# Fourier mixing and a maxout layer on one core: mirror rows stored by plain transfers, table columns in another order, and more units in split form

## The chip, the cores and the metric

The kernel runs on one core of a Trainium2 chip. The core has a matrix engine (TensorE, PE in the profile; its weight loads are listed as PEld), a vector engine (VectorE, DVE), a scalar engine (ScalarE, ACT), a general engine (GpSimd, POOL) and a sync engine (SyncE, SP), which here only issues transfers. DMA queues move data between the large memory and the on-chip memory; SP, ACT and POOL each issue transfers of their own. Each engine works through its own list of instructions in order and waits on semaphores for the others. Times are device microseconds of one execution; lower is better.

## What is computed

```python
def _attn_ref(x):                         # x: (8, 3072, 256)
    X = np.fft.fft(x, axis=1)
    X = np.fft.fft(X, axis=2)
    return X.real.astype(np.float32)

def _moe_ref(x, w1, w2, w3, w_out):       # x: (24576, 256), w1..w3: (256, 768), w_out: (768, 256)
    h = np.maximum(np.maximum(x @ w1, x @ w2), x @ w3)
    return (h @ w_out).astype(np.float32)
```

The result of the first, taken as 24576 rows of 256, goes into the second; the output is 24576 rows of 256 floats.

## The kernel before

The eight sequences (batches, b = 0 to 7) are worked on one after the other, each overlapped with the next. The transform along the sequence is made for half of the rows k only: for such a row the kernel holds an even part tE and an odd part tO (columns of two [128 x 1536] arrays), and the row k is formed with their sum, the mirrored row 3072 - k with their difference. So every column of tE and tO gives two output rows, called plus and minus, with two hidden arrays hp and hm.

**Making tE and tO (class Mix).** `s` multiplies the loaded x by a small table, `y` and `z` bring the product through the large memory into another layout (`db`, `yb`), `x` (method x0) fills in a column, and `k` makes 512 columns (a bank) of tE or tO from sine and cosine tables. `_parts` (lines 39 to 48) lists the pieces of a bank: each piece is one matmul with weights of its own, and its columns in the tables are 32 rows apart in k. `v` brings the first row of tO back as an array `vb`, spread over all partitions. These pieces for batch b + 1 are hung by a plan on the units of batch b.

**Units.** A batch has three blocks of 512 columns, and a block has six hidden chunks of 128 (NJC): 18 units, u = 0 to 17, and g = 18 b + u. The loop at line 855 goes through the units. A unit makes one chunk of hp and of hm: the largest of three products. One of them is taken out as a common term, so two remain, each with an even and an odd matmul.

- An ordinary unit: `begin` issues four matmuls (lines 490, 491) into two banks, ACT takes the positive part of one (`stmp`, line 503), DVE the maximum of both (hp, line 504). `finish` adds two matmuls by which both banks turn from plus to minus (line 497), and ACT and DVE do the same again (hm).
- A split unit (`is_split`): its third product is made two units earlier by `third` (lines 815 to 828) from one even and one odd matmul; ACT scales the odd one (line 823), DVE makes the even sum (line 824, which also reads vb), and POOL forms plus3 and minus3 (line 828). `begin` then issues two matmuls into one bank (lines 835, 836) and DVE takes the maximum with plus3 (line 837); `finish` adds one matmul to the same bank (line 497), and DVE takes the maximum with minus3 (line 849).

The order of both is what line 869 sets: if the unit before is a split one, it is finished ahead of this unit's begin; otherwise behind it. After begin and finish come `third` for two units ahead, `scatter`, ten steps of the output stage (`l2_some(10)`), and then the plan's pieces. Before the change the split units are the odd ones from g = 7 on: nine in a batch, six in batch 0.

**Output stage.** `l2_block` works on the block before in four pieces (sub 0 to 3) of 128 columns, 60 steps in six units. A piece gathers plus and minus in one bank `po` (lines 513, 536), and DVE adds the linear part (line 541) into a tile `ot` of [128 x 512], of which there are six: plus in the left half, minus in the right. SP stores the plus rows, two or three plain transfers a piece by `_runs`. The minus rows of a piece, whose place runs backwards, are written on POOL by an indirect transfer, one row per partition (line 622), with row numbers that `rows` computes in batch 0, and a one-element memset behind it (line 626). `l2_last` does the last block, where all other work is done: pieces in the order 3, 0, 1, 2, each with its stores spread over ACT, SP and POOL, and the last piece copied in two halves (line 574).

Of the kernel before, what the change touches and what calls it, by code (L numbers as in the profile page):

```python
# [29 lines left out]
def _runs(slot):  # L30

    if slot == 11:
        return [(0, 48, 0), (48, 96, 16), (96, 128, 15 + 32 * 64)]
    t, u = divmod(slot, 3)
    edge, r = 96 - 32 * u, 4 * t + 1 + u
    return [(0, edge, r + 32 * 32 * u), (edge, 128, r + 1)]


def _parts(g):

    cols = [(r, 96 * (r - 1), 96 if r < 15 else 64, 0) for r in range(1, 16)]
    cols += [(0, 1408, 48, 0), (16, 1456, 48, 0), (15, 1504, 32, 64)]
    done = []
    for (r, c, wd, _) in cols:
        a, z = max(c, 512 * g), min(c + wd, 512 * g + 512)
        if a < z:
            done.append(((r - 1) % 16 if r < 16 else 16, a - 512 * g, z - a))
    return done
# [3 lines left out]
def kernel(  # L52
# [62 lines left out]
    rows_m = consts.tile([128, 12 * B], INT32, tag="rows_m")  # L115
    mark = consts.tile([1, 1], FP32, tag="mark")
# [49 lines left out]
    kvec = gen.tile([128, NHALF + 1], FP32, tag="kvec")  # L166
    kv = kvec[:, 0:1440].rearrange("p (r j) -> p r j", j=96)

    def ramp(r):
        n = {0: 6, 6: 5, 11: 4}[r]  # L170
        iota(kv[:, r:r + n, :], [[1, n], [32, 96]], base=r + 1)

    dvec = gen.tile([128, 128], FP32, tag="dvec")
    for c, (s0, s1) in enumerate(FIRST):
        for h in range(2):
            load_x(0, s0, s1, h)
        if c == 0:
            iota(dvec, [[1, 128]])
        elif c < 3:
            ramp((0, 6)[c - 1])  # L180
# [12 lines left out]
    ramp(11)  # L193
    iota(kvec[:, 1408:1504].rearrange("p (r j) -> p r j", r=2), [[16, 2], [32, 48]])
    iota(kvec[:, 1504:NHALF], [[32, 32]], base=15 + 32 * 64)
    iota(kvec[:, NHALF:NHALF + 1], [[0, 1]], base=NHALF)
# [72 lines left out]
    q = gen.tile([128, NHALF + 1], FP32, tag="q")  # L269
# [118 lines left out]
    class Mix:  # L388
# [72 lines left out]
        def k(self, which, g, evict=nc.scalar.copy):  # L461

            tab = (te_tab, to_tab)[which]
            ps2 = ps_f.tile([128, 512], FP32, name="ps2", tag="ps")
            for (i, c0, wd) in _parts(g):
                nc.tensor.matmul(ps2[:, c0:c0 + wd], self.col(i, which),  # L466
                                 tab[:, g * 512 + c0:g * 512 + c0 + wd], start=True, stop=True)
# [38 lines left out]
    def stored(st, mine, others):  # L506
        for group in others:
            tc.declare_no_dep(st.ins, group=group, reason="each store has rows of its own")
        tc.add_to_no_dep_group(mine, st.ins)
# [7 lines left out]
    def l2_block(b, blk, hp, hm, te, to):  # L517

        base = b * S
        for sub in range(4):  # L520
            slot = blk * 4 + sub
            cp = slice(slot * 128, slot * 128 + 128)
            sp = slice(sub * 128, sub * 128 + 128)
            if sub % 2 == 0:
                pl = ps_f.tile([128, 512], FP32, name="pl", tag="ps")
                for i in range(2):
                    ci = (slot + i) * 128
                    nc.tensor.matmul(pl[:, i * 256:(i + 1) * 256], te[:, ci:ci + 128],  # L528
                                     gw[:, 0:256], start=True, stop=True)
                    yield  # L530
                even = even_pool.tile([128, 512], FP32, name="even", tag="even")
# [3 lines left out]
            ot = out_pool.tile([128, 512], FP32, name="ot", tag="ot")  # L535
# [5 lines left out]
            nc.vector.tensor_tensor(  # L541
                out=ot.rearrange("p (h c) -> p h c", h=2),
                in0=po.rearrange("p (h c) -> p h c", h=2),
                in1=lin.unsqueeze(1).to_broadcast([128, 2, 256]), op=ALU.add)
            lo = 1 if slot == 11 else 0
            waiting.append((b * 12 + slot, lo, ot))
            for (p0, p1, k0) in _runs(slot):
                row = base + k0
                stored(nc.sync.dma_start(out=out[row: row + 32 * (p1 - p0 - 1) + 1: 32, :],
                                         in_=ot[p0:p1, 0:256]), "direct", ("scattered",))  # L550

    def l2_last(hp, hm, te, to, flipped):

        base = (B - 1) * S
        ter, tor = flipped
        for sub in (3, 0, 1, 2):
# [4 lines left out]
            ot = out_pool.tile([128, 512], FP32, name="ot", tag="ot")  # L561
            for (h, tev, tov, wo, hid) in (
                    (0, te[:, cp], to[:, cp], gw[:, 256:512], lambda jc: hp[:, jc, sp]),
                    (1, ter[:, sm], tor[:, sm], gw[:, 512:768], lambda jc: hm[:, jc, sm])):
                if h == 0 or sub == 2:
# [7 lines left out]
                if sub == 2:  # L573
                    nc.vector.tensor_copy(out=ot[:, h * 256:(h + 1) * 256], in_=ph)
            if sub != 2:
                nc.vector.tensor_copy(out=ot, in_=po)
            stores = [(p0, p1, base + k0, 0) for (p0, p1, k0) in _runs(slot)]
            for (p0, p1, k0) in _runs(slot):
                if k0 == 0:
                    p0, k0 = 1, 32  # L580
                stores.append((128 - p1, 128 - p0, base + S - k0 - 32 * (p1 - p0 - 1), 256))
            for k, (p0, p1, row, c) in enumerate(stores):
                eng = (nc.scalar, nc.sync, nc.gpsimd)[(k + (sub == 2)) % 3]
                stored(eng.dma_start(out=out[row: row + 32 * (p1 - p0 - 1) + 1: 32, :],
                                     in_=ot[p0:p1, c:c + 256]), "direct", ("scattered",))

    def l2_mid():
# [20 lines left out]
        for _ in l2_hidden(po[0:B, 0:256], lambda jc: hmid[:, jc, :]):  # L608
            pass
        ot = out_pool.tile([128, 512], FP32, name="ot", tag="ot")  # L610
        nc.vector.tensor_copy(out=ot[0:B, 0:256], in_=po[0:B, 0:256])
        stored(nc.sync.dma_start(out=out[NHALF: NHALF + S * (B - 1) + 1: S, :],
                                 in_=ot[0:B, 0:256]), "direct", ("scattered",))
# [4 lines left out]
    def scatter():  # L618

        while waiting:  # L620
            at_row, lo, ot = waiting.pop(0)
            stored(nc.gpsimd.indirect_dma_start(  # L622
                out, bass.IndirectOffsetOnAxis(
                    ap=rows_m[0:128 - lo, at_row: at_row + 1], axis=0),
                ot[lo:128, 256:512], None), "scattered", ("scattered", "direct"))
            nc.gpsimd.memset(mark, 0.0)
# [60 lines left out]
    m.c(1, 7)  # L687
# [9 lines left out]
    def rows():  # L697

        rows_f = gen.tile([128, 12 * B], FP32, tag="rows_f")
        iota(rows_f.rearrange("p (b t u) -> p b t u", t=4, u=3), [[S, B], [-4, 4], [-1025, 3]],  # L700
             base=S - 1, cm=-32)
        rows_v = rows_f.rearrange("p (b r) -> p b r", r=12)
        adj = gen.tile([128, 12], FP32, tag="adj")
        adv = adj.rearrange("p (t u) -> p t u", u=3)
        four = pidx.to_broadcast([128, 4])
        pool = nc.gpsimd
        for u in range(3):
            scal(adv[:, :, u], four, float(96 - 32 * u), ALU.is_ge, 3071.0, ALU.mult, eng=pool)
        low = gen.tile([128, 2], FP32, tag="low")
        scal(low[:, 0:1], pidx, 47.0, ALU.is_ge, 1520.0, ALU.mult, eng=pool)  # L710
        scal(low[:, 1:2], pidx, 95.0, ALU.is_ge, -511.0, ALU.mult, eng=pool)
        scal(low[:, 0:1], low[:, 0:1], 2031.0, ALU.add, eng=pool)
        pool.tensor_tensor(out=adj[:, 11:12], in0=low[:, 0:1], in1=low[:, 1:2], op=ALU.add)
        pool.tensor_tensor(out=rows_v, in0=rows_v,
                           in1=adj.unsqueeze(1).to_broadcast([128, B, 12]), op=ALU.add)
        pool.tensor_copy(rows_m, rows_f)

# [5 lines left out]
    out_pool = ctx.enter_context(tc.tile_pool(name="outbuf", bufs=6))  # L723
# [45 lines left out]
    for (u, fn) in ((0, lambda: table(2, 512, 1024)), (0, lambda: m.c(7, 16)),  # L769
# [6 lines left out]
                    (3, lambda: table(2)), (3, lambda: table(0)), (5, rows),  # L776
# [28 lines left out]
    def is_split(g):  # L805
        return g % 2 == 1 and 7 <= g < B * UNITS
# [118 lines left out]
```

## Time and profile before

| | |
|---|---|
| median of three runs | 394.9 us (394.51 to 395.22) |
| the profiled execution, its own time | 395.75 us |
| its span in the profile | 393.8 us |
| clock granted to TensorE, mean | 0.996 |
| matrix engine busy | 377.7 us in 2710 instructions |
| vector / scalar / general engine busy | 315.0 / 263.0 / 332.9 us |
| transfers | 54.20 MB, 66901 packets |

The page of a profile gives the busy time of each engine, the chain of work that ended last (followed back from the last instruction, with its shares by engine and line), the costliest groups of instructions (line, engine, operation, output <- inputs, shape, count | busy us, mean ns of one | idle time of the engine before them and who ended it), and the DMA queues (packets, MB, share of the time of 16 DMA engines). A timeline row has start and length in us, engine, line, operation, count of merged instructions, and in brackets how long the engine had been idle and what ended that. Matmuls are pipelined: one of 512 columns is listed with 0.38 us, and the next starts earlier than that. Vector operations overlap a little in the same way. L150 is line 150 of the kernel.

### The profile page before, as it was taken

How to read it: one execution, taken by the hardware profiler on the slowest of the kernel's cores; microseconds unless marked ns; L12 is line 12 of the kernel's file. 1: busy time of each engine (PE TensorE's matmuls, PEld its weight loads, DVE VectorE, ACT ScalarE, POOL GpSimd, SP SyncE). 2: the span in 40 equal slices, each digit the busy share in tenths (PEclk: the TensorE clock that was granted, in tenths of full speed). 3: DMA queues.
4: the chain of work that ended last, by engine and by line, in shares of the span. 5: the costliest groups of instructions: out<-in, count | busy, mean ns of one | idle time of the engine just before them, and what ended most of it. 6: DMA issues, size and time to landing. Idle time of an engine off the chain costs nothing.

```text
span 393.8 us, 8383 instructions
## 1 busy us (share of the span) xinstructions
PE 377.7 (96%) x2710; PEld 235.9 (60%) x2759; DVE 315.0 (80%) x530; ACT 263.0 (67%) x476; POOL 332.9 (85%) x432
## 2 busy tenths in 40 slices
PE   6698999999999999999999999999999999999994
PEld 2354566566665666565665666556665666666673
DVE  7788897788687788788787888877887887887972
ACT  6877788677766887577867787578866447435420
POOL 8985698979978899889988899889977898869993
PEclk9999999999999999999999999999999999999998
DMA  7999576585838776495767876495333553321234
GB/s 115 159 194 183 131 191 146 114 191 150 161 102 144 190 153 144 117 206 137 137 150 120 210 132 160 118 206 124 108 108 101 131 147 90 94 77 47 90 96 131
DMA packets 66901, 54.20 MB, mean 138 GB/s; under 512 B 32702, under 2 KB 62556, under 8 KB 66003
## 3 DMA queue, kind: packets, MB, share of 16 engines
q0 software_dynamic: 24368, 26.53, 35.5%
q1 hardware_dynamic: 41978, 26.72, 27.0%
q8 instruction: 21, 0.34, 0.4%
q10 hardware_dynamic: 512, 0.43, 0.4%
q14 instruction: 22, 0.18, 0.1%
HBM read 36.95 MB, written 30.81 MB: 172 GB/s over the span
## 4 chain that ended last, share of the span: by engine, by line
PE 84%; DMA 4%; DVE 4%; ACT 3%; issue 2%; POOL 2%; SPq 1%; DVEq 0%; ACTq 0%; POOLq 0%
PE po L513 30%; PE pse L497 12%; PE pse L490 8%; PE pse L491 7%; PE po L536 4%; PE d L821 4%; PE pse L835 4%; PE e L819 3%; PE ps L466 3%; PE pse L836 3%; PE pl L528 2%; PE ps L401 2%; DMA yb<-db 2%; DMA xt<-in_x_dram 2%; ACT tb L405 1%
## 5 line engine op out<-in xcount | busy, mean ns | idle before, releaser
L503 ACT ACTIVATE stmp<-pse 128x512 bf16<-128x512 f32 x150 | 89.6, 600 | 66.1 <-PE pse L497 50.9
L622 POOL DMA_INDIRECT out_dram<-ot,rows_m x92 | 102.4, 1113 | 17.9 <-issue 8.8
L828 POOL TENSOR_TENSOR plus<-even,odd 128x512 bf16<-128x512 f32 x69 | 87.8, 1272 | 32.9 <-DVE even L824 32.7
L828 POOL TENSOR_TENSOR minus<-even,odd 128x512 bf16<-128x512 f32 x69 | 87.5, 1268 | 0.0
L513 PE MATMUL po<-wout_bf,hp 128*128 128x256 bf16 x576 | 86.1, 273 | 0.4
L837 DVE SCALAR_TENSOR_TENSOR hp<-pse,plus 128x512 bf16<-128x512 f32 x69 | 47.6, 689 | 46.5 <-PE pse L836 13.9
L513 PE MATMUL po<-wout_bf,hm 128*128 128x256 bf16 x576 | 78.6, 273 | 0.0
L513 PEld LDWEIGHTS <-hp 128*128 128x128 bf16 x576 | 56.4, 98 | 26.1
L497 PE MATMUL pse<-tO,gd_all 128*128 128x512 bf16 x217 | 70.5, 379 | 1.1 <-DVE hp L504 0.2
L513 PEld LDWEIGHTS <-hm 128*128 128x128 bf16 x576 | 56.4, 98 | 16.3
L541 DVE TENSOR_TENSOR ot<-po,even 128x512 f32<-128x512 f32 x92 | 62.7, 681 | 0.0
L504 DVE TENSOR_TENSOR hp<-pse,stmp 128x512 bf16<-128x512 f32 x75 | 51.4, 685 | 10.1 <-ACT stmp L503 8.7
L490 PE MATMUL pse<-tE,g_all 128*128 128x512 bf16 x148 | 56.0, 379 | 1.9 <-DVE tE L468 0.5
L504 DVE TENSOR_TENSOR hm<-pse,stmp 128x512 bf16<-128x512 f32 x75 | 51.5, 687 | 7.4 <-ACT stmp L503 4.1
L824 DVE SCALAR_TENSOR_TENSOR even<-vb,wcol,e 128x512 f32<-128x512 bf16 x69 | 50.8, 737 | 0.0
L491 PE MATMUL pse<-tO,g_all 128*128 128x512 bf16 x131 | 49.6, 379 | 0.2 <-issue 0.2
L849 DVE SCALAR_TENSOR_TENSOR hm<-pse,minus 128x512 bf16<-128x512 f32 x69 | 47.0, 681 | 0.7
L823 ACT ACTIVATE odd<-d 128x512 f32<-128x512 f32 x69 | 41.3, 598 | 6.2
L134 ACT COPY xt<-xt 64x762 bf16<-64x762 bf16 (+1 forms) x48 | 40.2, 838 | 1.1
L497 PEld LDWEIGHTS <-gd_all 128*128 128x128 bf16 x219 | 21.3, 97 | 22.2 <-issue 4.1
L536 PE MATMUL po<-gw,tO 128*128 128x512 bf16 x85 | 32.3, 380 | 0.0
L405 ACT CAST tb<-ps 128x512 bf16<-128x512 f32 x38 | 20.5, 588 | 14.1 <-PE ps L401 14.1
(175 smaller groups left out, 475.7 us busy)
## 6 DMA issues: line engine op xcount, KB each, us to landing
xt<-in_x_dram POOLq DMA_DIRECT2D x14, 384.0 KB, 8.4
out_dram<-ot SPq DMA_DIRECT2D x55, 96.0 KB
out_dram<-ot SPq DMA_DIRECT2D x64, 64.0 KB
db<-tb SPq DMA_DIRECT2D x21, 192.0 KB
vb<-vd SPq DMA_DIRECT2D x23, 128.0 KB
xt<-in_x_dram POOLq DMA_DIRECT2D x7, 400.0 KB, 6.9
xt<-in_x_dram POOLq DMA_DIRECT2D x7, 368.0 KB, 6.1
out_dram<-ot SPq DMA_DIRECT2D x62, 32.0 KB
```

The costliest lines, as they stand in the source:

```text
L490: nc.tensor.matmul(pse[:, 0:n], g_all[:, jc, 2 * i, :], te, start=True, stop=False)
L491: nc.tensor.matmul(pse[:, 0:n], g_all[:, jc, 2 * i + 1, :], to, start=False, stop=True)
L497: nc.tensor.matmul(pse, gd_all[:, jc, i, :], to, start=False, stop=True, skip_group_check=True)
L503: nc.scalar.activation(out=stmp[:, 0:n], in_=pses[0][:, 0:n], func=AX.Relu)
L504: nc.vector.tensor_tensor(out=dst, in0=src3, in1=stmp[:, 0:n], op=ALU.max)
L513: nc.tensor.matmul(po, hcols(jc), wout_bf[:, jc * 256:(jc + 1) * 256], start=False, stop=(jc == NJC - 1), skip_group_check=True)
L536: nc.tensor.matmul(po, to[:, cp], gw[:, 256:768], start=True, stop=True)
L541: nc.vector.tensor_tensor(out=ot.rearrange("p (h c) -> p h c", h=2), in0=po.rearrange("p (h c) -> p h c", h=2), in1=lin.unsqueeze(1).to_br ...
L622: stored(nc.gpsimd.indirect_dma_start(out, bass.IndirectOffsetOnAxis(ap=rows_m[0:128 - lo, at_row: at_row + 1], axis=0), ot[lo:128, 256:51 ...
L824: nc.vector.scalar_tensor_tensor(out=even3, in0=vb, scalar=wcol[:, jc:jc + 1], in1=e3, op0=ALU.mult, op1=ALU.add)
L828: nc.gpsimd.tensor_tensor(out=dst, in0=even3, in1=odd3, op=op)
L837: nc.vector.scalar_tensor_tensor(out=dst, in0=pse2, scalar=0.0, in1=sums[g][0], op0=ALU.max, op1=ALU.max)
```

## The change

Three things are changed.

1. *Order of the table's columns.* Each bank of 512 columns consists of four pieces of 128. In a piece, partition p of the output stage has in its first 96 places one residue of k (48 of a upper half, then 48 of a lower half, ascending in each), in the last 32 another one. Each `k` bank now has 8, 8 and 9 matmuls instead of 6, 6 and 8. The single leftover column is row 0 instead of row 1536.
2. *Stores.* A block's four pieces go into one buffer of [128 x 8 x 256], plus rows in places 0 to 3, minus rows in places 7 to 4, so that rows that follow one another in the output lie side by side. There are three such buffers (`obuf` and the two halves of `kq`, which holds the angles at the start). When the fourth piece is done, SP stores the plus rows with four transfers (six in the third block), and POOL the minus rows with two (three) plain transfers whose destination goes backwards in its inner dimension of 48 (or 16). The indirect transfers, `rows`, the memset and the six `ot` tiles are gone. In the last block the order of the pieces is 1, 2, 3, 0; the first three are stored together with twelve transfers, the last in two halves of four, all shared out over ACT, SP and POOL in turn.
3. *Split units.* Units 0, 4 and 8 of batches 1 to 7 are split as well: twelve in a batch, 90 in all instead of 69.

```diff
 def _parts(g):
-    cols = [(r, 96 * (r - 1), 96 if r < 15 else 64, 0) for r in range(1, 16)]
...
+    done = [(12 + i - 1, slice(128 * i + 96, 128 * i + 128)) for i in range(4)]
+    for i in range(4 if g < 2 else 3):
+        done.append((4 * g + i, slice(128 * i, 128 * i + 96)))
+    if g == 2:
+        done += [(16, slice(384, 480, 2)), (15, slice(385, 480, 2))]
     return done
...
-    kvec = gen.tile([128, NHALF + 1], FP32, tag="kvec")
+    kq = gen.tile([128, 4096], FP32, tag="kq")
+    kvec, q = kq[:, 0:NHALF + 1], kq[:, 2048:2049 + NHALF]
+    def ramp(g):
+        kv = kvec[:, 512 * g:512 * g + 512].rearrange("p (s c) -> p s c", s=4)
+        n = 4 if g < 2 else 3
+        iota(kv[:, 0:n, 0:96].rearrange("p s (a j) -> p s a j", a=2),
+             [[1, n], [-1536, 2], [32, 48]], base=4 * g + 1 + 1536)
+        iota(kv[:, :, 96:128].rearrange("p s (a j) -> p s a j", a=2),
+             [[1, 4], [-512, 2], [32, 16]], base=12 + 1024 * g + 512)
...
+    def back(v):
+        return v.rearrange("(a j) r d -> a j r d", a=2)[:, ::-1]
+    def stores_plus(b, blk, buf, s0=0, s1=4):
+        mine, v = rows_of(b)
+        n = s1 if blk < 2 else min(s1, 3)
+        for a in range(2):
+            j = 48 - 48 * a
+            yield v[j:j + 48, 4 * blk + 1 + s0:4 * blk + 1 + n, :], buf[48 * a:48 * a + 48, s0:n, :]
+            j = 32 * blk + 16 - 16 * a
+            yield v[j:j + 16, 12 + s0:12 + s1, :], buf[96 + 16 * a:112 + 16 * a, s0:s1, :]
+        if n < s1:
+            yield mine[784:784 + 46 * 16 + 1:16, :], buf[0:47, 3, :]
+            yield mine[16:16 + 47 * 16 + 1:16, :], buf[48:96, 3, :]
+    def stores_minus(b, blk, buf):
+        mine, v = rows_of(b)
+        n = 4 if blk < 2 else 3
+        r = 32 - 4 * blk
+        yield back(v[0:96, r - n:r, :]), buf[0:96, 8 - n:8, :]
+        yield back(v[64 - 32 * blk:96 - 32 * blk, 17:21, :]), buf[96:128, 4:8, :]
+        if n < 4:
+            yield back(mine[NHALF:S - 15:16, :].unsqueeze(1)), buf[0:96, 4:5, :]
...
             nc.vector.tensor_tensor(
-                out=ot.rearrange("p (h c) -> p h c", h=2),
-                in0=po.rearrange("p (h c) -> p h c", h=2),
+                out=buf[:, sub:8 - sub:7 - 2 * sub, :], in0=po.rearrange("p (h c) -> p h c", h=2),
                 in1=lin.unsqueeze(1).to_broadcast([128, 2, 256]), op=ALU.add)
...
+        for (dst, src) in stores_plus(b, blk, buf):
+            store(nc.sync, dst, src)
+        waiting.extend(stores_minus(b, blk, buf))
...
-        for sub in (3, 0, 1, 2):
+        for sub in (1, 2, 3, 0):
...
+                    if sub == 3:
+                        stores = [*stores_plus(B - 1, 2, buf, 1, 4),
+                                  *stores_turned(B - 1, buf, 1, 4)]
+                for k, (dst, src) in enumerate(stores):
+                    store((nc.scalar, nc.sync, nc.gpsimd)[k % 3], dst, src)
...
         while waiting:
-            at_row, lo, ot = waiting.pop(0)
-            stored(nc.gpsimd.indirect_dma_start(
...
-            nc.gpsimd.memset(mark, 0.0)
+            store(nc.gpsimd, *waiting.pop(0))
...
     def is_split(g):
-        return g % 2 == 1 and 7 <= g < B * UNITS
+        if g % 2 == 0:
+            return UNITS <= g < B * UNITS and g % UNITS in (0, 4, 8)
+        return 7 <= g < B * UNITS
```

`store` issues one transfer and declares that it has no dependence on the stores of the other two queues. `stores_turned` gives the minus rows of the last block, which `l2_last` computes in mirrored order, so that its transfers run forwards.

More of the change, by code (lines that the diff above doesn't have):

```diff
@@ L504, in unit_out, with store @@
         nc.vector.tensor_tensor(out=dst, in0=src3, in1=stmp[:, 0:n], op=ALU.max)
[L506 to L509, printed above, removed]
+    def store(eng, dst, src):
+        st = eng.dma_start(out=dst, in_=src)
+        for other in (nc.sync, nc.scalar, nc.gpsimd):
+            if other is not eng:
+                tc.declare_no_dep(st.ins, group=f"rows {other.engine}",
+                                  reason="each store has rows of its own")
+        tc.add_to_no_dep_group(f"rows {eng.engine}", st.ins)
@@ L609, in l2_mid @@
             pass
-        ot = out_pool.tile([128, 512], FP32, name="ot", tag="ot")
+        ot = even_pool.tile([128, 512], FP32, name="even", tag="even")
         nc.vector.tensor_copy(out=ot[0:B, 0:256], in_=po[0:B, 0:256])
-        stored(nc.sync.dma_start(out=out[NHALF: NHALF + S * (B - 1) + 1: S, :],
-                                 in_=ot[0:B, 0:256]), "direct", ("scattered",))
+        store(nc.sync, out[0: S * (B - 1) + 1: S, :], ot[0:B, 0:256])
     l2_queue = []
@@ L695 @@
     angle()
[L697 to L716, printed above, removed]
     ps_s_cm.__exit__(None, None, None)
@@ L767, in turn @@
         mirror(b, *EIGHTHS[ch])
[L769 removed]
+    for (u, fn) in ((0, lambda: table(2, 512, 1024)),
                     (0, lambda: next(second)), (0, lambda: next(first)),
```

95 lines of the change are left out of this document (38 added, 57 removed).

## The prediction, made before the changed kernel had run

> **What bounds the kernel now.** I read the page first: busy times, the chain of waits, the groups.
>
> ```profile
> span 393.8 us, 8383 instructions
> ...
> PE 377.7 (96%) x2710; PEld 235.9 (60%) x2759; DVE 315.0 (80%) x530; ACT 263.0 (67%) x476; POOL 332.9 (85%) x432
> ...
> PE 84%; DMA 4%; DVE 4%; ACT 3%; issue 2%; POOL 2%; SPq 1%; DVEq 0%; ACTq 0%; POOLq 0%
> ...
> L622 POOL DMA_INDIRECT out_dram<-ot,rows_m x92 | 102.4, 1113 | 17.9 <-issue 8.8
> L828 POOL TENSOR_TENSOR plus<-even,odd 128x512 bf16<-128x512 f32 x69 | 87.8, 1272 | 32.9 <-DVE even L824 32.7
> ```
>
> TensorE has work 96% of the span and carries 84% of the chain. GpSimd is next at 85%, a third of it the scattered mirror stores (1.11 us each), but it is hardly on the chain. Then a view by stretches: one steady batch, and one with the end of batch 0 and most of batch 1 (columns: length, then busy time and count for PE, weight loads, DVE, ACT, POOL, then clock, DMA share, GB/s).
>
> ```profile
> 212.44:257.35 44.91, 44.59 (x320) 27.95 (x325) 36.56 (x57) 32.92 (x59) 39.67 (x49) 1.00 0.70 151
> 45.00:122.62 77.62, 76.57 (x556) 48.03 (x566) 62.54 (x98) 57.88 (x102) 67.86 (x82) 1.00 0.64 146
> ```
>
> A batch takes 44.91 us, of which TensorE idles 0.32: removed matmul time is removed span, as long as no wait opens in its place. DVE looks free for 8.3 us in a batch. That is an average, so I looked at DVE where the new split units land, around the end of one batch (units 17 and 0, then 1).
>
> ```profile
> 157.05 0.69 DVE L837 SCALAR_TENSOR_TENSOR hp<-pse,plus 128x512 bf16<-128x512 f32 x1 [0.41 <-PE pse L836]
> 157.83 0.69 DVE L504 TENSOR_TENSOR hm<-pse,stmp 128x512 bf16<-128x512 f32 x1
> 158.43 0.74 DVE L824 SCALAR_TENSOR_TENSOR even<-vb,wcol,e 128x512 f32<-128x512 bf16 x1
> 159.09 0.68 DVE L541 TENSOR_TENSOR ot<-po,even 128x512 f32<-128x512 f32 x1
> 159.69 0.68 DVE L849 SCALAR_TENSOR_TENSOR hm<-pse,minus 128x512 bf16<-128x512 f32 x1
> 160.29 0.68 DVE L504 TENSOR_TENSOR hp<-pse,stmp 128x512 bf16<-128x512 f32 x1
> ```
>
> In order: hp of unit 17, hm of 16, the even sum for unit 1, the output add, hm of 17, hp of unit 0. From 157.83 on DVE is back to back, one start each 0.60 us (0.65 for the even sum), and hp of unit 0 starts when DVE gets to it, not when TensorE delivers. On TensorE in the same stretch:
>
> ```profile
> 158.74 0.38 PE L497 MATMUL pse<-tO,gd_all 128*128 128x512 bf16 x1
> ...
> 161.77 0.38 PE L819 MATMUL e<-tE,g_all 128*128 128x512 bf16 x1
> ```
>
> 158.74 is the start of unit 0 (the minus matmul of 17); 161.77 is the third() of unit 1, reached behind begin(1) and finish(0).
>
> **The change, part by part.** *The split of 21 more units* (0, 4 and 8 in seven batches). Each removes one 512-column matmul: six become five. Between the two rows above lie nine matmuls of 512 columns and ten steps of the output stage (in unit 0 one of 512 and eight of 256): 3.03 us for 14 x 512 columns, 0.216 us each. So the split is worth 21 x 0.216 = 4.5 us at most. Two of the five matmuls move two units ahead into third(). ACT loses one 0.6 us pass; POOL gains two of 1.27 us, DVE one even sum.
>
> What is left in unit 0 is short: finish(17) one matmul, begin(0) two, then ten steps of the output stage. Those ten take 5 x 0.216 = 1.08 us, so TensorE would be at finish(0) at 158.74 + 3 x 0.216 + 1.08 = 160.47. But a split unit is finished ahead of the next unit's begin, and finish(0) accumulates into the bank that hp(0) reads. hp(0) cannot start before 160.29 by the rows above, ends at 160.97, and the matmul follows about 0.06 us later, at 161.03: a wait of 0.56 us. Behind it on TensorE stand begin(1), third(3) and the output matmuls; DVE (hp of 1), ACT (odd sum) and POOL wait for those. With finish 0.216 and begin 0.43, third(3) starts at 161.68 instead of 161.77: 0.09 us won, against 0.43 us that third(0) adds in unit 16. Net +0.34 a batch instead of -0.22. The extra even sum in unit 16 doesn't make it worse: the 0.41 us gap in front of 157.05 and the 0.43 of TensorE take it up.
>
> Units 8 and 4, in the next batch's rows:
>
> ```profile
> 171.36 0.69 DVE L504 TENSOR_TENSOR hp<-pse,stmp 128x512 bf16<-128x512 f32 x1 [0.31 <-ACT stmp L503]
> ...
> 180.53 0.68 DVE L504 TENSOR_TENSOR hp<-pse,stmp 128x512 bf16<-128x512 f32 x1
> ...
> 182.01 0.38 PE L819 MATMUL e<-tE,g_all 128*128 128x512 bf16 x1
> ```
>
> Unit 8 has the same pattern (an add lies in unit 7): hp(8) at 180.53 is not preceded by a gap, finish(8) comes at 181.27, third(11) at 181.92 instead of 182.01, plus 0.43 for third(8): +0.34. I take +0.2, since TensorE waits already in units 9 and 10 (part of the 0.32 idle) and those waits give way; bounds -0.22 and +0.6, the latter where ACT's added odd sum (0.6) holds up hm(6). Unit 4 is different: its hp (171.36) waited 0.31 us for ACT, a wait that goes, so DVE is nearly in time: -0.11, bounds -0.22 and +0.1. Sum per batch 0.34 + 0.2 - 0.11 = 0.43, times seven: **+3.0 us**, bounds -4.5 (no wait at all) and +7.
>
> *The table in a new order* cuts each bank of the table product into 8, 8 and 9 pieces instead of 6, 6 and 8. A six-piece and an eight-piece group of before:
>
> ```profile
> 151.00 0.39 PE L466 MATMUL ps<-te_tab,yb 128*128 128x64 bf16 x6
> 151.23 0.38 PE L835 MATMUL pse<-tE,g_all 128*128 128x512 bf16 x1
> ```
> ```profile
> 153.62 0.41 PE L466 MATMUL ps<-to_tab,yb 128*128 128x32 bf16 x8
> 153.88 0.38 PE L497 MATMUL pse<-tO,gd_all 128*128 128x512 bf16 x1
> ```
>
> 0.23 against 0.26 us for the same 512 columns. The new groups have four pieces of 32 columns in a row, narrower than most here, so I take 0.27, 0.27 and 0.28: +0.10 a table, two tables, eight batches: **+1.7 us**; bounds +1.2 (0.26 for eight) and +2.2 (the stride-two pieces at half rate).
>
> *Mirror stores*: 92 scatters (1.11 us) and as many small memsets leave POOL, 53 plain stores come (0.53 us, below). With 3 x 2.54 us of new sums a batch, POOL goes from 39.7 to about 39.7 + 7.6 - 12 x 1.2 + 7 x 0.53 = 36.6 us: it is relieved, and as it isn't the bound, that gives nothing by itself. The `rows` arithmetic goes from batch 0. On SP, eight or nine stores of a block become four to six, all behind the block's last add, so in units 12 to 16 nothing stands in front of the small vd and vb transfers there. Buffers come round after three blocks (45 us); no wait. The stretch 45 to 122.6 idles 1.05 us, steady batches would idle 0.55 there; the 0.5 may go with the lighter queues: **-0.4**, bounds -0.5 and 0. The start: one more table instruction on POOL ahead of the first phase, **+0.1**, bounds 0 and 0.4.
>
> *The tail*:
>
> ```profile
> 387.36 2.67 SPq L584 DMA_DIRECT2D out_dram<-ot  x3
> 387.37 2.08 ACTq L584 DMA_DIRECT2D out_dram<-ot  x3
> ...
> 387.63 1.16 POOL L584 DMA_DIRECT2D out_dram<-ot  x2 [1.25 <-DVE ot L576]
> 388.46 0.42 DVE L574 COPY ot<-po 128x256 f32<-128x256 f32 x1 [0.52 <-PE po L513]
> ```
> ```profile
> L584 ACTq DMA_DIRECT2D out_dram<-ot x7: 375/428/534, 383.9 to 388.9; - x7
> ...
> L584 POOL DMA_DIRECT2D out_dram<-ot x5: 501/532/570, 384.5 to 388.2; - x5
> ```
>
> The last issue ends at 387.36 + 2.67 = 390.03, the span 3.8 us later. After the change twelve stores come after the third piece (at 387.37) and eight more after the halves of the last, shared as ACT 8, SP 6, POOL 6. ACT: 387.37 + 8 x 0.43 = 390.8; POOL: 387.63 + 6 x 0.53 = 390.8, where its last ended at 388.8. So +0.8 by ACT and up to 2 by POOL, whose stores end the span when they come last: **+1.3**, bounds 0 and 2.5.
>
> Sum: 3.0 + 1.7 - 0.4 + 0.1 + 1.3 = +5.7 us on the span, 399.5. The profiled execution took 395.75 (1.95 around its span), 0.85 over the median; on the median of 394.9 the forecast is **400.6 us**.
>
> **Rivals.** *DVE keeps up* (faster). For it: DVE is 19% idle, and with the batch it works 36.6 + 3 x 0.7 of 44.9 us. Against it: the gapless rows of units 17 and 7. If the waits don't open, the split gives its 4.5: -4.5 + 1.7 - 0.4 + 0.1 + 1.3 = -1.8, so 393.1. It decides from hp(0) starting 0.56 us earlier. Chance 0.22.
>
> *Half of it*: the waits take back what the split gives, and the rest is small: within 0.8 of 394.9. Chance 0.09.
>
> *The mirror stores run narrow.* Their destination has two as its outermost count. If such a store goes to two DMA engines only, 384 KB means 192 KB on each.
>
> ```profile
> q0 software_dynamic: 24368, 26.53, 35.5%
> q1 hardware_dynamic: 41978, 26.72, 27.0%
> ```
>
> A packet stream moved 26.53 MB in 35.5% of 16 x 393.8 us: 11.9 KB per us and engine on POOL's queue, 15.7 on the other. So 12 to 16 us for one store, where a block lasts 15. The last ordinary block's store is issued some 6 us ahead of the last copy (388.46) and lands 6 to 10 us after it, instead of 4 to 5. That puts 2 to 5.5 on the forecast: 404.5. It decides when that store lands after the last small ones. Against it: the loads on this queue have 32 outermost, so no row shows such a store. Chance 0.1. By the Trainium skill ("DMA: Bandwidth & Descriptors", section on why a DMA increments its semaphore by 16) the count of engines is the largest up to 16 that divides the slowest dimension of both sides, which would be two here; the page has an exception for some copies from GpSimd, and no run here shows which holds.
>
> *POOL's stores wait for one another* (the rows of two stores of a block interleave, and each is held until the one before has landed): POOL is blocked some 3 us for each of 30, the plus and minus sums come late, and DVE and TensorE wait for them: about 407. Against it: interleaved SP stores of before go out without such waits. Chance 0.09.
>
> **How the numbers follow.** Forecast 0.50, its own range 397.5 to 404; the rivals 0.22, 0.09, 0.1 and 0.09. No change is what lies within 0.2%, 0.8 us, about what a measurement of this kernel can tell. Faster 0.22 plus a little of the middle case, 0.23; same 0.09; slower 0.68. The range for 8 in 10 runs from 393.0 (half of the faster rival left out) to 405.5.
>
> **What would show it.** Right: the steady batch at 45.1 to 45.7 us, a TensorE wait of about 0.5 us on DVE's hp in front of the minus matmul of units 0 and 8, none at 4; table groups of 0.27 us; POOL under 37 us a batch; a last issue near 390.8 in relation to a last copy at 388.5. Wrong: a batch of 44.4 to 44.6 (DVE kept up), or hp of the split units waiting for POOL's plus. The prediction fails if DVE's chain from hm(16) to hp(0) is shorter than the 3.1 us that the rows show.

## The result, and the profile after

The changed kernel takes 439.8 us (median of 4 runs, 433.8 to 444.1), the kernel before in the same runs 395.0 (394.5 to 395.2). Two of the four, 440.7 and 444.1, lie over 1.5% above the fastest and count as slow, so that the ratio of 1.105 (interval 1.094 to 1.116) is that of the other two, 433.8 and 438.9. Their mean, 436.3 us, stands for the changed kernel in the differences below. Forecast were 400.6 us and a range up to 405.5. The direction was right, the size was not: +41 us, where +5.7 was expected.

The profiled execution is the fastest of the four, 433.8 us with a span of 432.0. From its page:

```profile
span 432.0 us, 8171 instructions
...
PE 383.7 (89%) x2769; PEld 238.6 (55%) x2818; DVE 330.4 (76%) x551; ACT 248.6 (58%) x454; POOL 308.2 (71%) x336
...
q0 software_dynamic: 39680, 26.67, 34.8%
...
PE 57%; DMA 21%; DVE 8%; issue 4%; ACT 3%; POOL 2%; SPq 2%; DVEq 0%; POOLq 0%; ACTq 0%
PE po L553 19%; DMA yb<-db 12%; PE pse L489 9%; DMA vb<-vd 4%; PE e L828 4%; PE pse L482 4%; PE d L830 3%; PE pse L483 3%; DMA vd<-tO 3%; PE pse L844 3%; PE po L576 3%; PE pse L845 3%; PE ps L393 2%; DVE hp L846 2%; DVE hm L858 2%
...
L499 POOL DMA_DIRECT2D out_dram<-kq x43 | 28.4, 666 | 5.8 <-DVE kq L614 3.6
```

POOL is relieved, as intended, and no engine is full. DMA has gone from 4% of the chain to 21%: 12 of it is the way of `db` into `yb`, 7 that of `tO` to `vd` to `vb`. That is what the next batch's table product and third products need. The waits of that kernel (who waited for what: us in total, times, longest) say it too:

```profile
ACT yb L447 <- DMA yb<-db: 20.7, 5, 7.0
...
PE ps L458 <- ACT yb L448: 13.5, 4, 5.5
...
PE pse L489 <- DVE hp L846: 9.1, 15, 1.2
...
DVE even L833 <- DMA vb<-vd: 7.9, 3, 3.0
```

Line 489 is the minus matmul that waits for hp, the wait that was forecast. The other three were not forecast, and the kernel before has only the first of them, with 1.4 us in all. Batches 3 to 6 of the same kernel, from unit 0 to unit 0 (columns as in the prediction):

```profile
172.75:220.50 47.75, 44.64 (x326) 27.96 (x331) 38.02 (x61) 30.71 (x55) 36.48 (x37) 1.00 0.67 142
220.50:271.98 51.48, 45.93 (x326) 28.45 (x331) 39.14 (x62) 30.82 (x55) 38.19 (x38) 0.97 0.60 132
271.98:325.81 53.83, 46.65 (x326) 28.86 (x331) 38.88 (x61) 30.82 (x55) 36.16 (x35) 0.94 0.48 112
325.81:371.28 45.47, 44.27 (x327) 27.99 (x332) 38.59 (x61) 24.21 (x46) 34.89 (x33) 1.00 0.46 114
```

Batch 6 takes 45.47 us, inside the forecast of 45.1 to 45.7. The batches before it take up to 8.4 us longer, and the clock falls with the waits (0.94). Nearly all of that lies in two units. In batch 5 the timeline shows the first matmul of unit 12 at 301.76, of unit 13 at 309.83 and of unit 14 at 315.32; in batch 6 the same two steps take 2.2 and 3.1 us, here 8.1 and 5.5. Unit 12 holds the first table product of the next batch, which needs `yb`. Its row, and that of the copy on ACT ahead of it:

```profile
309.14 0.23 ACT L447 CAST yb<-psx 128x16 bf16<-128x16 f32 x1 [7.03 <-DMA yb<-db]
...
309.42 0.61 PE L458 MATMUL ps<-to_tab,yb 128*128 128x32 bf16 x8 [5.55 <-ACT yb L448]
```

Now SP's queue in batches 5 and 6. Each row merges issues of one line; SP's time is that for which it was held by them:

```profile
280.63 6.33 SPq L415 DMA_DIRECT2D db<-tb  x4
287.06 7.36 SPq L499 DMA_DIRECT2D out_dram<-kq  x6
294.53 5.01 SPq L421 DMA_DIRECT2D yb<-db  x4
...
340.38 3.61 SPq L499 DMA_DIRECT2D out_dram<-kq  x6
344.09 1.72 SPq L421 DMA_DIRECT2D yb<-db  x4
```

In batch 5 six plus stores held SP for 7.36 us, in batch 6 for 3.61; the four transfers of `yb` behind them took 5.01 and 1.72. So the last part of `yb` was sent off at 299.54, 2.2 us ahead of unit 12; in batch 6 it was sent off at 345.81, 9.6 us ahead of unit 12 at 355.43. These 7.4 us are about the 7.03 that ACT waits for `yb`. SP's own instruction list is the same in both batches; what differs is what else is on its way, in batch 5 two loads of x that POOL issues at 276.12 and 279.11, right behind a pair of mirror stores, and in batch 6 none. The mirror stores on POOL's queue and the median of their times to landing:

```profile
out_dram<-obuf POOLq DMA_DIRECT2D x8, 384.0 KB, 12.8
out_dram<-kq POOLq DMA_DIRECT2D x8, 384.0 KB, 11.1
```

### The profile page after: what moved, and what is told of

Read it like the earlier page. It is cut to its first block, busy times and chain, and to the rows that moved or that the text cites. A ratio compares the mean times of both kernels' runs of the same rounds, so it can differ in the third digit from the quotient of the medians.

```text
span 432.0 us, 8171 instructions
## 1 busy us (share of the span) xinstructions
PE 383.7 (89%) x2769; PEld 238.6 (55%) x2818; DVE 330.4 (76%) x551; ACT 248.6 (58%) x454; POOL 308.2 (71%) x336
## 3 DMA queue, kind: packets, MB, share of 16 engines
q0 software_dynamic: 39680, 26.67, 34.8%
## 4 chain that ended last, share of the span: by engine, by line
PE 57%; DMA 21%; DVE 8%; issue 4%; ACT 3%; POOL 2%; SPq 2%; DVEq 0%; POOLq 0%; ACTq 0%
PE po L553 19%; DMA yb<-db 12%; PE pse L489 9%; DMA vb<-vd 4%; PE e L828 4%; PE pse L482 4%; PE d L830 3%; PE pse L483 3%; DMA vd<-tO 3%; PE pse L844 3%; PE po L576 3%; PE pse L845 3%; PE ps L393 2%; DVE hp L846 2%; DVE hm L858 2%
## 5 line engine op out<-in xcount | busy, mean ns | idle before, releaser
L837 POOL TENSOR_TENSOR plus<-even,odd 128x512 bf16<-128x512 f32 x90 | 114.4, 1271 | 105.6 <-DVE even L833 96.1
L837 POOL TENSOR_TENSOR minus<-even,odd 128x512 bf16<-128x512 f32 x90 | 114.1, 1268 | 0.0
L495 ACT ACTIVATE stmp<-pse 128x512 bf16<-128x512 f32 x108 | 64.6, 601 | 26.4 <-PE pse L483 11.3
L833 DVE SCALAR_TENSOR_TENSOR even<-vb,wcol,e 128x512 f32<-128x512 bf16 x90 | 66.4, 738 | 7.9 <-DMA vb<-vd 7.9
L858 DVE SCALAR_TENSOR_TENSOR hm<-pse,minus 128x512 bf16<-128x512 f32 x90 | 61.7, 685 | 11.8 <-PE pse L489 10.2
L496 DVE TENSOR_TENSOR hp<-pse,stmp 128x512 bf16<-128x512 f32 x54 | 37.2, 689 | 26.7 <-ACT stmp L495 22.5
L581 DVE TENSOR_TENSOR kq<-po,even 128x512 f32<-128x512 f32 x60 | 41.0, 684 | 0.1
L482 PE MATMUL pse<-tE,g_all 128*128 128x512 bf16 x100 | 37.9, 379 | 0.7 <-DVE tE L460 0.4
L828 PE MATMUL e<-tE,g_all 128*128 128x512 bf16 x89 | 34.5, 387 | 3.2 <-DVE even L833 2.9
L830 PE MATMUL d<-tO,gd_all 128*128 128x512 bf16 x90 | 34.9, 387 | 0.2
L499 POOL DMA_DIRECT2D out_dram<-kq x43 | 28.4, 666 | 5.8 <-DVE kq L614 3.6
```

Source lines behind the costliest of these rows:

```text
L482: nc.tensor.matmul(pse[:, 0:n], g_all[:, jc, 2 * i, :], te, start=True, stop=False)
L495: nc.scalar.activation(out=stmp[:, 0:n], in_=pses[0][:, 0:n], func=AX.Relu)
L496: nc.vector.tensor_tensor(out=dst, in0=src3, in1=stmp[:, 0:n], op=ALU.max)
L828: nc.tensor.matmul(e3, g_all[:, jc, 2, :], te, start=True, stop=True)
L833: nc.vector.scalar_tensor_tensor(out=even3, in0=vb, scalar=wcol[:, jc:jc + 1], in1=e3, op0=ALU.mult, op1=ALU.add)
L837: nc.gpsimd.tensor_tensor(out=dst, in0=even3, in1=odd3, op=op)
```

## The experiments

The theory: a mirror store, with two as its destination's outermost count, goes to two DMA engines only (the third rival of the prediction); SP's transfers, which need those engines too, are held up, and `yb` and `vb` come late. The rivals: the negative step itself, the bunched plus stores ahead of `yb` on SP's queue, and the added split units.

**Forward destinations.**

```diff
     def back(v):
-        return v.rearrange("(a j) r d -> a j r d", a=2)[:, ::-1]
+        return v
```

> The mirror rows of all blocks but the last are stored with their destination going forwards, so that its outermost count is 96 (or 32) instead of two; count, bytes, queue and moment of the stores stay, the mirror rows land in each other's places. Narrow stores (a store with two outermost uses two DMA engines, takes 11 to 13 us, and holds up the transfers of yb and vb behind it): the landings of POOL's stores drop from 11-13 us to under 8, the TensorE waits of 1.7 to 5.7 us ahead of the table product in unit 12 and of 1.5 us at the third product that needs vb go, a batch takes 45.2 to 45.8 us, and the time is 397 to 404 us. Bunched plus stores on SP's queue ahead of yb's transfers: nothing changes, 432 to 445. Too many split units: nothing changes either, 432 to 445.

Measured: 402.4 us (402.1 to 402.5), 1.018 times the kernel before (1.016 to 1.020). SP's queue in batch 5 of that run, and two of its landings:

```profile
266.72 3.56 SPq L499 DMA_DIRECT2D out_dram<-kq  x6
270.38 1.41 SPq L421 DMA_DIRECT2D yb<-db  x4
```

```profile
out_dram<-obuf POOLq DMA_DIRECT2D x8, 384.0 KB, 6.4
out_dram<-kq POOLq DMA_DIRECT2D x8, 384.0 KB, 3.5
```

34 of the 41 us are gone, SP's issues are as quick as in batch 6 of the changed kernel, and no wait for `yb` is left. What remains is close to the forecast.

**Forward, but two or four outermost.**

```diff
-        return v
+        return v.rearrange("(j a) r d -> a j r d", a=2)     # second kernel: a=4
```

> As the run with forward destinations, but the 96 (or 32) rows are taken as two interleaved sets, outermost count two, inner count 48 (or 16), still forwards. Narrow stores: as slow as the changed kernel, 430 to 447 us, landings 11 to 13 us. If the negative step itself were what costs (descriptors that are slow to make or to write), it would be as fast as the forward run, 397 to 404 us.

> Forward destinations taken as four interleaved sets: outermost count four, between two (438.4 us) and 96 (402.4 us); the mirror rows land in each other's places. Narrow stores: four engines a store, so the landings fall from 11-13 us to some 6 to 8, SP's issues are held up for half as long, and the time lies between, 403 to 418 us. If the outermost count were not what sets the number of engines (interleaving itself being slow): 430 to 445 us.

Measured: 438.4 us (437.0 to 438.9) with two, 404.3 (403.9 to 406.2) with four. Landings of 384 KB stores, first with two outermost, then with four:

```profile
out_dram<-obuf POOLq DMA_DIRECT2D x8, 384.0 KB, 12.9
```

```profile
out_dram<-obuf POOLq DMA_DIRECT2D x8, 384.0 KB, 8.7
out_dram<-kq POOLq DMA_DIRECT2D x8, 384.0 KB, 7.2
```

The negative step costs nothing that can be seen; the interleaving, which the run with four has too, costs little. The outermost count is what matters. By the Trainium skill ("DMA: Bandwidth & Descriptors", section on why a DMA increments its semaphore by 16) the count of engines is the largest up to 16 that divides the slowest dimension of both sides: 2, 4 and 16 for the three forms. The landings agree (12.9, 8.7, 6.4 us for the same bytes), and the page's exception for some copies from GpSimd does not hold for these.

No view names the DMA engine of a packet, but the traces have each packet's time. Take the two mirror stores of one block (512 KB) in batch 6, which POOL issues at 358.18 in the changed kernel, at 330.74 with four outermost and at 330.00 with forward destinations. In all three they are 128 packets of 4 KB, of 0.20, 0.22 and 0.20 us each. With two outermost at most 5 of them are under way at a time (2.5 on average), and they take 10.0 us; with four at most 8 (4.8), 5.9 us; with forward destinations up to 18 (7.9), 3.3 us. So a narrow store's packets are not slower, there are fewer of them at a time.

Four is nearly enough (1.9 us above the forward run): the harm does not grow in proportion to the landing time. Where between 8.7 and 12.9 us it sets in, no run shows.

**The split units of before** (`is_split` as in the kernel before, all else changed).

```diff
     def is_split(g):
-        if g % 2 == 0:
-            return UNITS <= g < B * UNITS and g % UNITS in (0, 4, 8)
-        return 7 <= g < B * UNITS
+        return g % 2 == 1 and 7 <= g < B * UNITS
```

> The changed kernel with the split units of before (nine in a batch, 69 in all). Narrow stores: the waits for yb and vb stay, and the three split units give or take no more than 3 us, so 430 to 445 us. Too many split units (TensorE waiting for DVE's and POOL's added work, which makes all later steps late): nearly all of the 45 us goes, 396 to 401 us.

Measured: 446.2 us (441.4 to 454.0). Not the split units: without the new ones even the two fastest runs, 441.4 and 443.2, are no faster than the changed kernel. ACT's wait for `yb` is 40.6 us there instead of 20.7.

**Plus stores behind `yb`'s transfers.** Their issue is put off to the end of the first unit with u % 6 other than 0.

```diff
-        for (dst, src) in stores_plus(b, blk, buf):
-            store(nc.sync, dst, src)
+        late.extend(stores_plus(b, blk, buf))
...
+        while late and u % NJC != 0:
+            store(nc.sync, *late.pop(0))
```

> The changed kernel with the plus stores of a block issued two units later on the same queue, behind the transfers of yb in units 6 and 7 and behind the first vd and vb transfers in units 12 and 13. Bunched plus stores: yb's transfers are issued some 5 us sooner, the TensorE waits ahead of the table product go, 398 to 406 us. Narrow stores: yb is issued sooner, which takes off part of its wait, while vb still waits for two busy DMA engines: 415 to 440 us.

Measured: 412.9 us (409.9 to 414.1). The plus stores of the last block but one (512 KB) are never issued in this kernel, so it flatters a little. The result lies between the two expectations: the order on SP's queue carries some 23 of the 34 us that narrow stores cost, and does so only beside narrow stores, since with wide ones the old order leaves no wait for `yb` (402.4). A wait of up to 4.0 us for `vb` is left.

**Mirror stores cut by row,** with the split units of before.

```diff
-        yield back(v[0:96, r - n:r, :]), buf[0:96, 8 - n:8, :]
-        yield back(v[64 - 32 * blk:96 - 32 * blk, 17:21, :]), buf[96:128, 4:8, :]
+        for i in range(n):
+            yield back(v[0:96, r - n + i:r - n + i + 1, :]), buf[0:96, 8 - n + i:9 - n + i, :]
+        for i in range(4):
+            yield back(v[64 - 32 * blk:96 - 32 * blk, 17 + i:18 + i, :]), buf[96:128, 4 + i:5 + i, :]
```

> The changed kernel with the split units of before and with each mirror store cut by row: four stores of one row a group (or three) instead of one of four, backwards and with two as the outermost count as before, eight a block. Compared with 446.2 us for the split units of before alone. Narrow stores that take engines in turn: eight stores are spread over up to sixteen engines, each engine has at most 96 KB instead of 192 KB, the landings drop to 4 to 8 us, SP's six plus stores and yb's transfers go out in time, 397 to 408 us. Narrow stores that always take the same two engines: nothing won, 440 to 455. The size of a store or its row runs (4 KB runs become 1 KB) as the cause: slower still, above 446.

Measured: 440.1 us (428.1 to 443.8). The expectation of 397 to 408 fell: the fastest run is still 20 us above it, although the landings dropped to about 7 us. Three waits of the profiled run, which took 443.8 us:

```profile
DVE hp L846 <- POOL plus L837: 50.8, 19, 4.1
...
ACT yb L447 <- DMA yb<-db: 25.7, 5, 10.6
...
POOL out_dram L499 <- DMA xt<-in_x_dram: 10.1, 5, 3.7
```

Eight issues in a row hold POOL for 5.3 us, and at times POOL stands in front of its seventh or eighth store until a load has come in; its sums come late (50.8 us), and `yb` is late still. Cutting a narrow store into narrow stores was no cure here; how far the engines were shared out better can't be told from this run.

**Without the loads of x.** Batch 6 of the changed kernel has narrow stores and no wait; it is also the first batch in which no x is loaded.

```diff
-            if b > 2:
+            if False:
                 at(b - 3, (9 + (b == 3), 11, 18, 19)[ch], lambda b=b, ch=ch: fetch(b, ch))
```

> The changed kernel without the loads of x for batches 3 to 7 (those batches work on x that is already in the chip; 20 transfers of 368 to 400 KB on POOL's queue are left out). The narrow mirror stores stay. Narrow stores that hold up the others by themselves: the waits for yb and vb in batches 1 to 5 stay, 425 to 445 us. Narrow stores that do it only together with the loads of x, which queue behind them on POOL's queue (batch 6, the first without such loads, had no wait): all batches like batch 6 (45.5 us), 401 to 408 us.

Measured: 408.4 us (407.5 to 409.8). No wait for `yb` is left, and two for `vb`, 2.0 us in all, though the stores land nearly as late as in the changed kernel:

```profile
out_dram<-obuf POOLq DMA_DIRECT2D x8, 384.0 KB, 11.9
```

So the waits in the middle need both, the narrow stores and the loads of x. Whether the loads matter because they stand behind the stores on the same queue, or only for the 8 MB that they move, this run doesn't tell apart. The end doesn't need them: here it is 5 us longer than with forward destinations (from unit 0 of batch 7 to the end of the span, 62.5 against 57.5 us).

**What the new split units cost.** Four runs: forward destinations with the split units of before; the kernel before with the new split units; and each form with a split unit finished behind the begin of the next one.

```diff
-        if prev is not None and is_split(prev[0]):
+        if prev is not None and is_split(prev[0]) and not is_split(g):
             finish(*prev)
```

> Forward destinations (mirror rows in each other's places) with the split units of before; beside 402.4 us with the new split units. From undisturbed batches of the runs so far (45.47 us with the new split units, 44.84 without), the new split units cost 0.63 us in each of seven batches, 4.4 us: 398.0, range 397 to 399.5. If the split units were worth what they save on TensorE, it would be 404 to 407.

> The kernel before with the new split units and nothing else. By the same 0.63 us a batch 399.3, range 397.5 to 401. DVE keeps up (TensorE saves 4.5 us): 390 to 392.

> The kernel before with the new split units, and with a split unit that is followed by another split one finished behind the begin of that one, not ahead of it, so that DVE has two more matmuls (0.43 us) of time for hp. If TensorE's wait for hp in front of the minus matmul (0.55 to 0.99 us a time) is what makes the split units lose: 394 to 397.5, below the run before it by 2 to 5 us. If DVE's queue as a whole is what is full in those units, or POOL's sums come late: no better than 399.

> Forward destinations, the new split units, and a split unit that is followed by another split one finished behind the begin of that one, so that DVE has two more matmuls of time for hp. Beside 402.4 us (new split units, finished ahead) and 396.6 (split units of before). If TensorE's waits for hp in front of the minus matmul are what makes the new split units lose: 394 to 399 us. If DVE is full there in any order: 401.5 to 404.

Measured: 396.6 us (396.2 to 396.9) for the first, so the new split units cost 402.4 - 396.6 = 5.8 us beside wide stores. Finished later, 404.2 (403.6 to 405.1): the wait only changes its place. TensorE's waits on DVE in the profiles of both forward runs, first finished ahead, then behind:

```profile
PE pse L489 <- DVE hp L846: 6.3, 13, 0.7
```

```profile
PE pse L844 <- DVE hm L858: 6.4, 13, 0.7
```

In the first TensorE waits for hp before the minus matmul, in the second for hm before the begin of a later unit: the order of two matmuls doesn't help. That DVE as a whole is full in those units is what remains, and its rows at unit 0, shown further down, stand back to back. In the kernel before, the new split units give 430.8 us (429.2 to 433.6), with the later finish 433.9 (432.2 to 434.0), where 399.3 was expected of the first. One batch of the first, and one of its waits:

```profile
220.05:270.95 50.90, 46.32 (x322) 28.26 (x321) 38.84 (x61) 30.91 (x55) 47.16 (x54) 0.97 0.61 134
```

```profile
DVE hp L839 <- POOL plus L830: 32.3, 20, 3.4
```

POOL has 47.2 us of work in a batch that took 44.9 before: beside the scatters, the new sums fill POOL, and hp waits for them. As POOL's sums set the pace there, the later finish could show nothing.

**Unit 4 alone in the kernel before.** (`g % UNITS in (4,)`)

> The kernel before with unit 4 of batches 1 to 7 split and nothing else: the only one of the three new split units that did not make TensorE wait in the runs so far (units 2 to 6, without the third product of unit 8, 0.13 us shorter a batch). If that holds beside the scatters: 7 x 0.13 = 0.9 us less than before, 393.6 to 394.7. If GpSimd, which has 39.7 us of work in a batch of 44.9 and gets 2.5 more, delivers its sums late (as with all three new split units beside the scatters, 430.8): 396 to 407.

Measured: 399.9 us (399.1 to 400.0), 1.012 times the kernel before (1.010 to 1.013). In batch 4 unit 6 starts 10.35 us behind unit 2, 0.13 less than before, as hoped; but unit 9 takes 3.77 us instead of 2.67. DVE's hp waits 22.2 us in all for POOL's plus there, and POOL has 42.2 us of work in a batch.

**Stores piece by piece at the end,** forward destinations, split units of before.

```diff
-                    if sub == 3:
-                        stores = [*stores_plus(B - 1, 2, buf, 1, 4),
-                                  *stores_turned(B - 1, buf, 1, 4)]
+                    stores = [(dst, src) for (dst, src) in
+                              [*stores_plus(B - 1, 2, buf, sub, sub + 1),
+                               *stores_turned(B - 1, buf, sub, sub + 1)] if 0 not in src.shape]
```

> Forward destinations, the split units of before, and in the last block the stores of each piece issued as soon as it is copied, not those of three pieces together. Beside 396.6 us. If the twelve stores at once behind the third piece make the end late (7.4 us from the last copy to the end, where the kernel before had 4.9): 393.5 to 395.5. If not: 396 to 397.5.

Measured: 397.5 us (397.4 to 398.5), no gain over 396.6. The bunching of twelve stores is not what lengthens the end.

No version beat the kernel before. The nearest, forward destinations with the split units of before, is 0.25% slower (1.001 to 1.004), and it writes the mirror rows into each other's places: the forward runs show what wide stores would cost, and are not kernels to use.

## Why the prediction was wrong

Three stretches of the span tell where the time lies: up to unit 0 of batch 1, from there to unit 0 of batch 7, and the rest. The kernel before, the forward run, the changed kernel:

```profile
0.00:68.56 68.56, 60.37 (x448) 35.18 (x457) 55.84 (x124) 53.17 (x103) 56.31 (x98) 1.00 0.92 160
68.56:338.62 270.06, 267.86 (x1909) 167.59 (x1944) 218.91 (x342) 190.89 (x341) 234.15 (x282) 1.00 0.63 142
338.62:393.80 55.18, 49.49 (x356) 33.12 (x360) 40.27 (x66) 18.92 (x33) 42.48 (x53) 0.97 0.30 87
```

```profile
0.00:70.20 70.20, 62.72 (x469) 36.18 (x478) 56.93 (x125) 53.70 (x103) 49.75 (x82) 1.00 0.87 148
70.20:343.10 272.90, 264.79 (x1949) 167.82 (x1985) 230.21 (x360) 179.16 (x323) 213.04 (x216) 1.00 0.61 141
343.10:400.60 57.50, 48.51 (x352) 32.69 (x355) 42.03 (x68) 16.42 (x29) 36.01 (x39) 0.97 0.34 93
```

```profile
0.00:71.72 71.72, 63.14 (x469) 36.28 (x478) 56.09 (x123) 54.14 (x104) 49.36 (x81) 1.00 0.85 144
71.72:371.28 299.56, 271.95 (x1950) 169.61 (x1986) 232.37 (x362) 178.00 (x321) 221.32 (x217) 0.98 0.58 129
371.28:432.00 60.72, 48.61 (x352) 32.71 (x355) 41.93 (x68) 16.42 (x29) 37.54 (x39) 0.93 0.35 88
```

With wide stores the change costs 1.64 + 2.84 + 2.32 = 6.8 us of span; the sum of the prediction was 5.7. With narrow ones 3.2 + 29.5 + 5.5 = 38.2 in the profiled run. So the sum was nearly right for all that it held, though in part by luck: the split units cost more than was put down, and relieving POOL gave back about as much where nothing was put down (both below). The step that failed by far the most is one:

*The narrow stores were priced at the tail alone* ("It decides when that store lands after the last small ones", +2 to +5.5 us, chance 0.1). The mechanism was there, and so was its size: 12 to 16 us were worked out for a landing, 11 to 13 came. But it was followed to the last block only. The same kind of store goes out in every block before. With loads of x on their way too, SP's issues slow to half their pace (7.36 against 3.56 us for six), `yb` comes late, and TensorE waits at the table product. That is 436.3 - 402.4 = 33.9 us, or 438.4 - 402.4 = 36.0 by the outermost count alone, about nine times the price given (404.5 against 400.6). The tail's own part of it, 5.5 - 2.3 = 3.2 us, is what had been priced; the rest, 29.5 - 2.8 = 26.7 us in the profiled runs, lies in batches 1 to 6. What inside the DMA engines or SP's queue slows the issues is not seen in any view and stays open. In the sum the same blind spot stands twice: "lighter queues" were booked as a gain of 0.4, and "nothing stands in front of the small vd and vb transfers" looked at the order on SP's queue alone, and not at the narrow stores that are on their way then. `yb`, behind six plus stores in unit 6, was not looked at.

The other terms, in order:

- *The waits for hp in units 0 and 8, none at 4: right, and mis-sized in sum.* Batch 6 of the changed kernel at unit 0 (DVE, then TensorE):

```profile
326.55 0.68 DVE L858 SCALAR_TENSOR_TENSOR hm<-pse,minus 128x512 bf16<-128x512 f32 x1
327.15 0.68 DVE L846 SCALAR_TENSOR_TENSOR hp<-pse,plus 128x512 bf16<-128x512 f32 x1
```

```profile
326.68 0.82 PE L553 MATMUL po<-wout_bf,hp 128*128 128x256 bf16 x6
327.88 0.38 PE L489 MATMUL pse<-tO,gd_all 128*128 128x512 bf16 x1 [0.39 <-DVE hp L846]
```

  DVE's order is the one forecast, hm of 17 and then hp(0), back to back. Six steps of 0.11 from 326.68 end at 327.33, and the minus matmul starts at 327.88: a wait of 0.55 us, forecast 0.56 (the row's 0.39 counts from the listed end of the matmul before). Unit 4 won 0.13 us in the run with it alone (forecast 0.11). Over the whole run the new split units cost 5.8 us instead of 3.0, still inside the bounds of -4.5 to +7. In batch 4 it is 0.79 (45.62 with them, 44.83 without, from unit 0 to unit 0); over batches 1 to 6 it is 272.90 - 268.95 = 3.95 us, 0.66 a batch, instead of 0.43. Another 1.4 us lies ahead of unit 0 of batch 1 (70.20 against 68.80 without them), where unit 0's third product falls into the end of batch 0; that was not counted, though 0.5 of it is there at unit 0 of batch 0 already, ahead of any split unit.
- *The table's order*, +1.7: units 12 to 17 of batch 4 (first matmul of unit 12 to that of the next unit 0) take 15.42 us in the forward run with the split units of before, 15.16 in the kernel before. 0.26 in each of seven batches are 1.8 us: right. The groups of eight take 0.27 us there and those of nine 0.30, where 0.27 and 0.28 were forecast.
- *POOL relieved, worth nothing by itself*: not quite. In the same two profiles units 9 and 10 take 4.55 us against 4.90 before; if every batch is like this one, about 0.35 a batch, 2.5 us in all, come back. That is the gain that hides the 2.8 us by which the split units were priced too low. And the new split units rest on it: with the scatters still on POOL they cost 36 us.
- *The start*, +0.1: 68.80 against 68.56 without the new split units, +0.24.
- *The tail*, +1.3 with bounds 0 and 2.5: +2.3 with wide stores, +5.5 with narrow ones. Its rows in the changed kernel:

```profile
414.41 13.80 SPq L499 DMA_DIRECT2D out_dram<-kq  x10
414.68 1.34 POOL L499 DMA_DIRECT2D out_dram<-kq  x2 [2.24 <-DVE kq L581]
...
418.13 8.88 ACTq L499 DMA_DIRECT2D out_dram<-kq  x8
...
420.96 0.42 DVE L610 COPY kq<-po 128x256 f32<-128x256 f32 x1 [0.52 <-PE po L553]
```

  SP is still issuing at 428.2, 6.8 us behind the last copy. The issues were priced at 0.43 us each; behind the two narrow stores of 414.68, eight of ACT's take 8.88 us. What makes the end 2.3 us longer with wide stores stays open: issuing the stores piece by piece didn't help.

Of the other rivals, DVE didn't keep up, and POOL's stores didn't wait for one another (0.67 us a store).

## What to carry to other kernels

A transfer's outermost count is a price of its own, and here it was paid by other transfers, not where the narrow one was issued. When a store looks narrow, follow its landing time through the whole steady state, and list what is in flight meanwhile that somebody waits for, with the slack that each has: here `yb` had room for a quiet queue only. And before splitting work onto an engine, add up its load per batch, with what the rest of the change takes off it: the same edit cost 6 us with GpSimd relieved and 36 us without.

## What the runs showed of the hardware

- The loss is not in proportion to the narrowness. Kernels whose stores of 384 KB landed in 11 to 13 us took 36 us longer than the one with wide ones, and with landings in 7 to 9 us 2 us longer (438.4, 404.3, 402.4).
- Narrow stores and loads on one queue come with slower issuing on another engine's queue: six plus stores took SP 7.36 us beside narrow stores and loads of x, 3.61 beside narrow stores in a batch without such loads, 3.56 with wide stores.
- A narrow store comes with many more packets for the same bytes: 39680 on POOL's queue in the changed kernel, of which 21112 have 4 to 16 bytes; in the forward run 20304, of which 1680 have:

```profile
q0 software_dynamic: 20304, 26.57, 34.9%
```
